# Three more products joined two by two in a nested Strassen-Winograd feed-forward

## The chip, the cores and the metric

The kernel runs on one core of a Trainium2 chip. The metric is the device time of one execution in microseconds; before the change the median of three runs is 378.93 us (378.29 to 379.14).

## What is computed

```python
def _attn_ref(q, k, v):                       # 8 batches, 12 heads, 448 tokens, 64 wide
    scores = np.matmul(q, k.transpose(0, 1, 3, 2)) / np.sqrt(q.shape[-1])
    attn = np.exp(scores - np.max(scores, axis=-1, keepdims=True))
    attn = attn / (np.sum(attn, axis=-1, keepdims=True) + 1e-09)
    return np.matmul(attn, v)

def _moe_ref(x, w_in, w_out):                 # x: 3584 x 768, w_in: 768 x 2048, w_out: 2048 x 768
    h = x @ w_in
    g = h * (1.0 / (1.0 + np.exp(-h)))
    return g @ w_out
```

The attention's output, heads side by side, is the x of the second function.

## The kernel before

**Stages.** Attention runs over 24 units of four heads. The first feed-forward product gives G, the gated hidden values, with 128 hidden columns on the partitions in each of 16 blocks f. For batches 0 to 3 it is done batch by batch with tanh gates, for the pairs of batches 4, 5 and 6, 7 by Winograd's seven products (`pair_product`, tiles `f`, three 448-column matmuls per product) with sums `sx` of x and `tw` of w_in; ScalarE then writes G with Silu. The second product, G times w_out, is done over 28 tiles of 128 tokens, two at a time: a *quad* qd holds tiles 2qd and 2qd+1, and there are 14 (0 to 13).

**A quad** is again Winograd: tokens in two tiles, hidden blocks in two halves of eight, output columns in two halves of 384 (`OH`). Its seven products (`product`, L924) take eight 128x384 matmuls each. Products 1, 2, 4 and 7 take G itself or sums written over it, products 5, 6 and 3 take sums S that VectorE makes (`combine_g`, L907, two halves of 128x512 each: S5, S6, G7, S3). The right sides are w_out or its differences D4, D5, D6. Products 1, 6, 7 and 4 share one PSUM bank and 5 and 3 another (`BANK`, L920): the bank goes on adding while readings of it are taken. ScalarE copies the bank after 1, 5, 6 and 4 into four fp32 outputs (`take_copy`, L1005), and VectorE adds the bank to them after 2, 7 and 3 (`take_sum`, L1023), which completes an output and stores it. So product 5 goes into two outputs: into (1,1), which is completed by 7, and, because product 3 is added on top of it in its bank, into (0,1), which is completed by 3.

**Joined products.** Product m of two quads a and b is twice a 128 x 1024 by 1024 x 384 product with the same right side. `FOLD` (L255) lists where both are taken together as one 2 x 2 problem with seven products of quarter size (`fold_product`, L1086): four 128x192 matmuls each, 28 in place of two times eight 128x384 ones. The price is four sums of the left sides (`fold_x`, L1064, tiles `fold`), four sums of the right side once for each m (`fold_w`, L1055, tiles `right` and others), and five readings of two banks P and Q (`fold_read`, L1109) in place of two readings. Before the change product 4 is joined for quads 7 and 8, 10 and 11, and 12 and 13, and product 2 for 10 and 11. A pair in `AHEAD_OF` runs before its quads' other products; its first readings are then copies by ScalarE (readings 1, 6, 5), and its result is added at the end by `take_last` (L1018). Entries of `FOLD` from index `MID` = 2 on take ordinary banks m for P and Q, the first two take the two double banks s that the scores used before.

**What sets the order.** The order of all engines is worked out while the program is built, by a list scheduler (`Order`, L111). Each operation has a duration written into the code, and `start` (L133) frees VectorE after that duration less `OVERLAP` (0.07). VectorE takes the ready operation with the smallest sum of ready time and bias: readings have -4, S sums 0, x and weight sums 1. TensorE takes the first entry of the list `moe` that is ready (`moe_ready`, L1938, which looks at 80 entries); quads stand in it in their order, each product as eight entries (`queue_quad`, L1796), and a joined product as seven (`queue_fold`, L1702). Buffers are counted as rings: four banks m, two or three s, three S tiles (`sg_ring`), and the output tiles of a quad (`home_of`, L1277: quads 8 and 10 use `wide` tiles, 11 others of that kind, 12 four `ost` tiles, 13 old xT tiles). `plan_sums` (L1618) plans S sums quad by quad once all of the quad's gates are known, `plan_folds` (L1657) the sums of joined products. On the chip each engine follows its queue in that order and waits for what is not there yet.

Quads 7 to 9 lie between the two pairs, from 280 us on; quads 10 to 13 need the last pair and run from 336 us to the end. The last product is product 2 of quad 13, in two halves of 192 columns (`p_2` and `p_2r`).

Of the kernel before, what the change touches and what calls it, by code (L numbers as in the profile page):

```python
# [9 lines left out]
FP16 = mybir.dt.float16  # L10
# [204 lines left out]
def kernel(  # L215
# [36 lines left out]
    FAR = (NT * B // 4 - 1,)  # L252
    BROAD = NT * B // 4 - 3
    WIDE = (NT * B // 4 - 6, NT * B // 4 - 4)
    FOLD = ((10, 11, (2, 4)), (12, 13, (4,)), *((7, 8, (4,)),))  # L255
    MID = 2
    AHEAD_OF = ((1, 4),)
    LEAD = 0
    TAIL = None
    folded = {(q, m) for a, b, ms in FOLD for q in (a, b) for m in ms}  # L260
# [645 lines left out]

    def combine_g(qd, m, f0, f1):  # L907
        a, b = 2 * qd, 2 * qd + 1
        if m != 7 and (qd, m) not in S_t:
# [8 lines left out]
        nc.vector.tensor_tensor(out=dst[:, f0:f1], in0=x[:, f0:f1], in1=y[:, f0:f1], op=op)  # L918
# [2 lines left out]

    half_t = {}

    def product(qd, m, f0, f1, strips, c0=0, c1=OH):  # L924
        w = {1: rows(2 * qd, 0), 2: rows(2 * qd, 1), 4: rows(2 * qd + 1, 1), 7: rows(2 * qd + 1, 0)}
        w = w[m] if m in w else S_t[(qd, m)]
        if BANK[m] == m and f0 == 0:
            pr_t[(qd, m)] = psum_bank(f"p_{qd}_{m}" + "r" * (c0 > 0))
        if c1 - c0 < OH:
            half_t[c0] = pr_t[(qd, m)]  # L930
        for f in range(f0, f1):
            times(
                pr_t[(qd, BANK[m])][:, 0 : c1 - c0],
                w[:, f, :],
                W_[m][:, f, c0:c1],
                f == 0 and BANK[m] == m,
                f == HF - 1,
                strips,
            )
# [70 lines left out]
    def take_end(p, c0, c1):  # L1010
# [3 lines left out]
        for lo, eng in ((0, nc.sync), (64, nc.scalar)) if c0 else ((0, nc.sync),):  # L1014
            hi = lo + 64 if c0 else 128
            eng.dma_start(out=out[row + lo : row + hi, c0:c1], in_=t[lo:hi])

    def take_last(qd):  # L1018
        t = ost_t[(qd, *OUT[4])]
        nc.vector.tensor_tensor(out=t, in0=bank(qd, 1), in1=t, op=ALU.add)  # L1020
        store(qd, *OUT[4])
# [7 lines left out]
    x2_t, n2_t = {}, {}  # L1029

    def left(q, m, k):
        return rows(2 * q + m // 4, 1)[:, 4 * k : 4 * k + 4]

    def right(m, k, j):
        return W_[m][:, 4 * k : 4 * k + 4, OH // 2 * j : OH // 2 * (j + 1)]
# [72 lines left out]

    def fold_read(g, m, k):  # L1109
        a, b = FOLD[g][:2]  # L1110
        i, j = {2: SUM[2], 4: OUT[4]}[m]
        bank = n2_t[(g, m, "P" if k in (1, 6, 7) else "Q")]
        q = b if k in (7, 5) else a
        if (g, m) in AHEAD_OF and k in (1, 5):
            ost(q, i, j)
        t = ost_t[(q, i, j)]
        if (g, m) in AHEAD_OF and k in (1, 6, 5):
            at = slice(0, OH) if k == 5 else slice(OH // 2 * (k // 6), OH // 2 * (k // 6 + 1))
            nc.scalar.copy(out=t[:, at], in_=bank[:, 0 : at.stop - at.start])
            return  # L1120
        if k in (1, 6):
            at = slice(OH // 2 * (k // 6), OH // 2 * (k // 6 + 1))
            nc.vector.tensor_tensor(out=t[:, at], in0=bank[:, 0 : OH // 2], in1=t[:, at], op=ALU.add)
        elif k == 7:
            v = t.rearrange("p (j n) -> p j n", j=2)
            nc.vector.tensor_tensor(
                out=v,
                in0=bank[:, 0 : OH // 2].unsqueeze(1).to_broadcast([128, 2, OH // 2]),
                in1=v,
                op=ALU.add,  # L1130
            )
            if (g, m) not in AHEAD_OF:
                store(b, i, j)
        else:
            nc.vector.tensor_tensor(out=t, in0=bank[:, 0:OH], in1=t, op=ALU.add)
            if k == 2 and (g, m) not in AHEAD_OF:
                store(a, i, j)
# [121 lines left out]
    def take_bank(name):  # L1259
        bank_of[name] = m_ring.take()  # L1260
# [357 lines left out]
    def plan_sums():  # L1618

        if not quads:  # L1620
            return
        qd, todo = quads[0]
        if len(todo) == 4:
            gates = {}
            for f in range(NFF):
                gates[f] = gates_at(2 * qd, f) + gates_at(2 * qd + 1, f)
                if None in gates[f]:
                    return
            gates_of[qd] = gates
# [22 lines left out]
        if not todo:  # L1652
            quads.pop(0)
# [3 lines left out]
    def plan_folds():  # L1657

        last = PAIRS[1]
        if "w" not in w2_op and last_pair and e_ring.can(1, od.now):  # L1660
            w2_op["w"] = True
            e_slot["spare"] = e_ring.take()
            for m in (4, 2):
                for i in (1, 2, 3, 4):
                    more = [w2_op[(m, i // 2)]] if i in (2, 4) else []
                    w2_op[(m, i)] = od.add(
                        Op("DVE", 0.57, lambda m=m, i=i: fold_w(m, i), last_pair + more, 1)
                    )
        if not folds or "w" not in w2_op:
            return  # L1670
        g, m, done = folds[0]
        made = [x for q in FOLD[g][:2] for f in range(HF, NFF) for x in gates_at(2 * q + m // 4, f)]
        n = len(x2_op) // 4
        if g < MID:
            if (last, HF - 1) not in pair_done:
# [26 lines left out]
    def queue_fold(g, m):  # L1702
# [1 line left out]
        done, reads = {}, {}  # L1704
        fold_done.append(done)
        folds.append((g, m, done))
        first = {2: 1, 4: 4}[m]
        early = (g, m) in AHEAD_OF
        if early:
            ahead[a] = lambda: when([reads.get(2)])  # L1710
            ahead[b] = lambda: when([reads.get(7)])
        home = {q: home_of(q) for q in (a, b)}

        def read(k, busy, deps, then=None):
# [4 lines left out]
        def queue(k):  # L1719
# [48 lines left out]
            def deps():  # L1768
# [15 lines left out]
                if not i:  # L1784
# [11 lines left out]
    def queue_quad(qd):  # L1796
# [16 lines left out]
        def queue(m, f0, f1, c0=0, c1=OH):  # L1813
            first = {6: (1,), 2: (1,), 7: (6, 5), 3: (5, 6) if qd == LAST else (5, 6, 7), 4: (7,)}.get(m, ())

            def run():
# [7 lines left out]
                if BANK[m] == m and f0 == 0:  # L1824
                    take_bank(f"p_{qd}_{m}" + "r" * (c0 > 0))
                for ring, need in rings:
                    ring.take(need)
                if m in (5, 6, 3) and f1 == HF:
# [8 lines left out]
                    od.add(Op("DVE", 0.33, fn, [op, took[1]], -4))  # L1837
                    return
                pr_op[(qd, m)] = op
                read(m, [op] + [took[x] for x in {2: (1,), 7: (5,), 3: (6,)}.get(m, ())])  # L1840
                if m == 7 and (qd, 4) in folded:
                    if qd in ahead:
                        def then(at):
                            leave_bank(f"p_{qd}_1")(at)
                            home.give(at + STORE)
# [6 lines left out]
                                [op, took[7], ahead[qd]],  # L1852
                                -4,
                                then=then,
                            )
# [4 lines left out]
            def deps():  # L1860
# [4 lines left out]
                made += [took.get(x) if x in hard else (took.get(x), 9.0) for x in first]  # L1865
                if m in (1, 2, 4):
                    t = 2 * qd + m // 4
                    i = int(m != 1)
# [6 lines left out]
            rings = ((home, 1),) if f0 == 0 and (m in OUT or m == 7 and (qd, 4) in folded and qd not in ahead) else ()  # L1875
            moe.append((deps, int(BANK[m] == m and f0 == 0), run, rings))


        begun = {}
# [460 lines left out]
```

## Time and profile before

| | |
|---|---|
| median of three runs | 378.93 us |
| the profiled execution | 378.17 us |
| its span, first to last instruction | 376.4 us |
| granted TensorE clock | 1.000 |
| TensorE busy | 370.2 us, 98% |
| VectorE busy | 287.5 us, 76% |
| ScalarE busy | 255.6 us, 68% |
| chain that ended last | PE 95%, ACT 3%, DMA 1% |

PE is TensorE's matmuls, PEld its weight loads, DVE is VectorE, ACT ScalarE, POOL GpSimd and SP the queue that issues most stores. The page divides the span into 40 slices of 9.4 us and gives the busy share of each engine in tenths. In lists in order of time a line merges equal instructions: start, length from the first start to the last end, engine, line, output and inputs, shape and count; an idle time in front of it and what ended it stand in brackets. Instructions of one engine overlap, so that the distance from one start to the next is shorter than the length of a line that holds one instruction.

### The profile page before, as it was taken

To read this page: it belongs to the slowest core of one execution; us is meant where nothing else is said; L and a number is where in the kernel's file an instruction comes from. 1 tells how busy PE (TensorE), PEld (TensorE's weight loads), DVE (VectorE), ACT (ScalarE), POOL (GpSimd) and SP (SyncE) were. 2 spreads that over 40 slices of the span, in tenths; PEclk is the share of its full clock that TensorE was granted. 3 is DMA by queue.
4 is the path that set the end of the run, shared out by engine and by line. 5 is a ranking of instruction groups with operands and counts; after the bars stand their busy time and mean duration, and the time that the engine had idled before them with its cause. 6 is when DMAs were issued, how large, how long until landed. Compare 5 with 4: busy or idle time off the path is not lost.

```text
span 376.4 us, 9978 instructions
## 1 busy us (share of the span) xinstructions
PE 370.2 (98%) x4030; PEld 188.0 (50%) x4030; DVE 287.5 (76%) x597; ACT 255.6 (68%) x401; POOL 85.0 (23%) x155
## 2 busy tenths in 40 slices
PE   7999999999999999999999999999999999999996
PEld 3365445444444444444444454545556655556764
DVE  3668858999995969995969998899379725449853
ACT  4988873896878787877788777658872238883130
POOL 6653337424016326006423200000000000000000
PEclk9999999999999999999999999999999999999999
DMA  7999999919049849147954411210002240001334
GB/s 113 198 208 209 207 200 181 205 21 132 16 96 153 154 51 123 27 94 108 176 91 67 57 46 44 55 32 0 0 3 53 74 108 20 0 1 34 84 96 126
DMA packets 35966, 34.47 MB, mean 92 GB/s; under 512 B 11856, under 2 KB 35152, under 8 KB 35920
## 3 DMA queue, kind: packets, MB, share of 16 engines
q0 software_dynamic: 25312, 22.82, 40.9%
q1 hardware_dynamic: 10064, 10.38, 10.1%
q10 hardware_dynamic: 544, 0.64, 0.5%
q8 instruction: 31, 0.51, 0.5%
q14 instruction: 15, 0.12, 0.1%
HBM read 45.61 MB, written 11.01 MB: 150 GB/s over the span
## 4 chain that ended last, share of the span: by engine, by line
PE 95%; ACT 3%; DMA 1%; DVE 0%; issue 0%; POOLq 0%
PE p L685 29%; PE h L685 21%; PE f L685 16%; PE s L448 11%; PE a L570 8%; PE o L685 3%; ACT E L504 2%; PE a L556 2%; PE a L603 2%; PE n_Q L685 1%; PE n_P L685 1%; DMA rk<-in_k_dram 1%; ACT T L493 1%; PE z L685 0%; PE p_2r L685 0%
## 5 line engine op out<-in xcount | busy, mean ns | idle before, releaser
L504 ACT ACTIVATE E<-s 128x896 f16<-128x896 f32 x164 | 141.9, 921 | 24.5 <-PE s L448 24.5
L685 PE MATMUL h<-xT,w_in_t 128*32 128x448 f16 (+2 forms) x762 | 83.5, 348 | 0.0
L685 PEld LDWEIGHTS <-w_in_t 128*128 128x128 f16 (+1 forms) x909 | 54.6, 97 | 50.0 <-issue 8.0
L354 POOL DMA_DIRECT2D V<-in_v_dram x88 | 48.5, 560 | 51.2 <-PE a L570 29.2
L685 PEld LDWEIGHTS <-G 128*128 128x128 f16 (+1 forms) x668 | 41.9, 97 | 28.0 <-issue 5.2
L717 ACT ACTIVATE th<-h 128x448 f16<-128x448 f32 x67 | 36.6, 546 | 24.2 <-PE h L685 20.7
L685 PE MATMUL p<-w_out_t,G 128*128 128x384 f16 (+2 forms) x326 | 51.8, 324 | 0.0
L448 PE MATMUL s<-rq,KT 32*128 32x448 f16 (+3 forms) x728 | 44.9, 347 | 1.4 <-DVE rq L412 0.9
L685 PEld LDWEIGHTS <-S 128*128 128x128 f16 (+1 forms) x321 | 29.5, 98 | 22.3 <-issue 3.4
L761 DVE SCALAR_TENSOR_TENSOR G<-th,h 128x448 f16<-128x448 f16 (+1 forms) x64 | 35.7, 573 | 4.8 <-ACT th L717 4.3
L685 PE MATMUL p<-D,S 128*128 128x384 f16 (+1 forms) x217 | 39.0, 326 | 0.0
L1006 ACT COPY ost<-p 128x384 f32<-128x384 f32 x38 | 18.2, 480 | 24.6 <-PE p L685 16.2
L570 PE MATMUL a<-E,V 128*32 128x448 f16 (+1 forms) x640 | 32.7, 356 | 0.0
L1025 DVE TENSOR_TENSOR ost<-p,ost 128x384 f32<-128x384 f32 x29 | 16.0, 553 | 18.4 <-ACT ost L1006 9.6
L673 DVE SCALAR_TENSOR_TENSOR xT<-a,rdn 128x448 f16<-128x448 f32 x46 | 27.0, 619 | 3.0 <-PE a L570 2.4
L334 POOL DMA_DIRECT2D rq<-in_q_dram x25 | 13.9, 559 | 67.3 <-PE s L448 57.9
L448 PEld LDWEIGHTS <-KT 32*128 32x128 f16 (+1 forms) x824 | 12.3, 96 | 31.5 <-issue 29.8
L517 DVE TENSOR_TENSOR T<-T,E 128x1792 f16<-128x1792 f16 x21 | 22.8, 1086 | 4.7 <-ACT E L504 4.7
L888 DVE TENSOR_TENSOR p<-f,p 128x448 f32<-128x448 f32 x15 | 9.4, 624 | 22.2 <-PE f L685 12.3
L517 DVE TENSOR_TENSOR T<-E,E 128x1792 f16<-128x1792 f16 x21 | 22.8, 1084 | 4.0 <-ACT E L504 4.0
L685 PE MATMUL f<-sx,tw 128*128 128x448 f16 x102 | 23.4, 352 | 0.0
L570 PEld LDWEIGHTS <-V 128*32 128x32 f16 (+1 forms) x640 | 13.5, 95 | 18.0 <-issue 10.1
(134 smaller groups left out, 464.5 us busy)
## 6 DMA issues: line engine op xcount, KB each, us to landing
out_dram<-ost SPq DMA_DIRECT2D x147, 48.0 KB, 1.8
rk<-in_k_dram POOLq DMA_DIRECT2D x24, 224.0 KB, 5.4
rq<-in_q_dram POOLq DMA_DIRECT2D x23, 224.0 KB, 5.7
w_out_t<-in_moe_w_out_dram POOLq DMA_DIRECT2D x4, 768.0 KB, 13.5
V<-in_v_dram POOLq DMA_DIRECT2D x42, 64.0 KB, 4.0
out_dram<-wide SPq DMA_DIRECT2D x48, 48.0 KB, 1.6
V<-in_v_dram POOLq DMA_DIRECT2D x42, 48.0 KB, 4.4
w_in_t<-in_moe_w_in_dram POOLq DMA_DIRECT2D x6, 256.0 KB, 8.7
```

What stands on the lines that cost most here:

```text
L334: nc.gpsimd.dma_start(out=rawq[n][:, cols], in_=group_of(q, b, hg)[:, cols])
L354: nc.gpsimd.dma_start(out=VT[b][32 * x : 32 * (x + 1), hs, at : at + count, :], in_=v[b, hs].rearrange("h (i g) d -> i h g d", g=TPP)[:, : ...
L448: nc.tensor.matmul(out=pS[p0 : p0 + 32 * (x1 - x0), h % 2, at : at + q1 - q0], lhsT=KT[(b, hg)][32 * h : 32 * (h + 1), key_rows(b, hg, c, ...
L504: nc.scalar.activation(out=E[(n, w)][:, 2 * y : 2 * y + 2, :], in_=pS_t[(n, w, y)][:, :, 0:S], func=AF.Exp, scale=attn_scale,)
L517: nc.vector.tensor_tensor(out=T[n], in0=T[n] if step else E[(n, 0)], in1=E[(n, step + 1)], op=ALU.add,)
L570: nc.tensor.matmul(out=a[32 * h : 32 * (h + 1), 0:S], lhsT=VT[b][k0:k1, HG * hg + h, place(b, hg, c), part - 1 :: 2], rhs=e[k0:k1, h], sta ...
L673: nc.vector.scalar_tensor_tensor(out=x3(b, cc)[:, cc % 3, 32 * g0 : 32 * g1], in0=acc[(n, part)][:, 0:nq], scalar=0.5, in1=rdn_t[n].rearra ...
L685: nc.tensor.matmul(out=out[i : i + cut], lhsT=w[:, i : i + cut], rhs=x, start=start, stop=stop, skip_group_check=True,)
L717: nc.scalar.activation(out=th, in_=h_t[(b, f, t0)][:, 0:n], func=AF.Tanh)
L761: nc.vector.scalar_tensor_tensor(out=dst[:, f, at + lo : at + hi], in0=th_t[(b, f, t0)][:, lo - t0 : hi - t0], scalar=1.0, in1=h_t[(b, f, ...
L1006: nc.scalar.copy(out=ost(qd, *OUT[m]), in_=bank(qd, BANK[m]))
L1025: nc.vector.tensor_tensor(out=t, in0=bank(qd, BANK[m]), in1=t, op=ALU.add)
```

## The change

`FOLD` gets product 5 of quads 10 and 11, product 5 of quads 12 and 13, and product 2 of quads 8 and 9 (a new entry with index 3). Both products 5 run ahead of their quads.

- Sums S5 of quads 10 to 13 do not take a tile S any more but an old tile of 448 columns by four heads: that of `tw_4_4`, `tw_3_0`, `tw_4_0` and `sx_6_3` (sums that the last pair's products read). They take no place in `sg_ring`.
- The sums of the right side for m = 5 are written over columns 0 to 767 of w_in, planned when the last pair's blocks f = 0 to 5 have all been multiplied.
- With 5 joined, product 3 opens its own bank (`opens`). The result of the joined product lies in output (1,1); `take_mix` adds it on VectorE to output (0,1), which the copy after product 6 has filled. Readings 7 and 3 wait for that.
- Durations that the planner charges: an S sum after the scores are done 0.35 instead of 0.40, an x sum 0.36 instead of 0.43.

```diff
-    FOLD = ((10, 11, (2, 4)), (12, 13, (4,)), *((7, 8, (4,)),))
+    FOLD = ((10, 11, (5, 2, 4)), (12, 13, (5, 4)), (7, 8, (4,)), (8, 9, (2,)))
     MID = 2
-    AHEAD_OF = ((1, 4),)
+    AHEAD_OF = ((0, 5), (1, 5), (1, 4))
...
+        if m == 5 and (qd, 5) in folded:
+            slot = e_slot[{10: "tw_4_4", 11: "tw_3_0", 12: "tw_4_0", 13: f"sx_{PAIRS[1]}_3"}[qd]]
+            if (qd, m) not in S_t:
+                t = sb.tile([128, HG, S], FP16, name=f"S_{qd}_{m}", tag=f"E{slot}", bufs=1)
...
+    def opens(qd, m):
+        return BANK[m] == m or m == 3 and (qd, 5) in folded
...
+    def take_mix(qd):
+        t = ost_t[(qd, *OUT[6])]
+        nc.vector.tensor_tensor(out=t, in0=t, in1=ost_t[(qd, *OUT[5])], op=ALU.add)
...
+        if m == 5:
+            return w_in_t[:, i - 1, 0 : 2 * OH].rearrange("p (f n) -> p f n", f=4)
...
-        while todo and (todo[0] == 7 or sg_ring.can(1, od.now)):
+        while todo and (todo[0] == 7 or (qd, todo[0]) in folded or sg_ring.can(1, od.now)):
             m = todo.pop(0)
-            if m != 7:
+            if m != 7 and (qd, m) not in folded:
                 sg_ring.take()
...
-                            0.40,
+                            0.40 if qk_seq else 0.35,
...
+        if "five" not in w2_op and (last, 5) in pair_done:
+            made = [pair_done[(last, f)].get(m) for f in range(6) for m in range(1, 8)]
+            if None not in made:
+                w2_op["five"] = True
+                for i in (1, 2, 3, 4):
+                    more = [w2_op[(5, i // 2)]] if i in (2, 4) else []
+                    w2_op[(5, i)] = od.add(Op("DVE", 0.57, lambda i=i: fold_w(5, i), made + more, 1))
...
-                Op("DVE", 0.43, lambda i=i: fold_x(g, m, i, homes[i - 1]), made + more, 1)
+                Op("DVE", 0.36, lambda i=i: fold_x(g, m, i, homes[i - 1]), made + more, 1)
...
-                read(m, [op] + [took[x] for x in {2: (1,), 7: (5,), 3: (6,)}.get(m, ())])
+                read(m, [op] + [took[x] for x in {2: (1,), 7: (5,), 3: (6,) + (5,) * ((qd, 5) in folded)}.get(m, ())])
+                if m == 6 and (qd, 5) in folded:
+                    took[5] = od.add(
+                        Op("DVE", OH / 960.0 + 0.13, lambda: take_mix(qd), [took[6], ahead[(qd, 5)]], -4)
+                    )
```

More of the change, by code (lines that the diff above doesn't have):

```diff
@@ L908, in combine_g @@
         a, b = 2 * qd, 2 * qd + 1
-        if m != 7 and (qd, m) not in S_t:
+        if m == 5 and (qd, 5) in folded:
+            slot = e_slot[{10: "tw_4_4", 11: "tw_3_0", 12: "tw_4_0", 13: f"sx_{PAIRS[1]}_3"}[qd]]
+            if (qd, m) not in S_t:
+                t = sb.tile([128, HG, S], FP16, name=f"S_{qd}_{m}", tag=f"E{slot}", bufs=1)
+                t = t.rearrange("p h s -> p (h s)")[:, 0 : 128 * HF]
+                S_t[(qd, m)] = t.rearrange("p (f t) -> p f t", f=HF)
+        elif m != 7 and (qd, m) not in S_t:
             S_t[(qd, m)] = sb.tile([128, HF, 128], FP16, name=f"S_{qd}_{m}", tag="S", bufs=NSG)
@@ L926, in product @@
         w = w[m] if m in w else S_t[(qd, m)]
-        if BANK[m] == m and f0 == 0:
-            pr_t[(qd, m)] = psum_bank(f"p_{qd}_{m}" + "r" * (c0 > 0))
+        if opens(qd, m) and f0 == 0:
+            pr_t[(qd, BANK[m])] = psum_bank(f"p_{qd}_{BANK[m]}" + "r" * (c0 > 0))
         if c1 - c0 < OH:
@@ L935, in product @@
                 W_[m][:, f, c0:c1],
-                f == 0 and BANK[m] == m,
+                f == 0 and opens(qd, m),
                 f == HF - 1,
@@ L1031, in left @@
     def left(q, m, k):
-        return rows(2 * q + m // 4, 1)[:, 4 * k : 4 * k + 4]
+        x = S_t[(q, 5)] if m == 5 else rows(2 * q + m // 4, 1)
+        return x[:, 4 * k : 4 * k + 4]
     def right(m, k, j):
@@ L1110, in fold_read @@
         a, b = FOLD[g][:2]
-        i, j = {2: SUM[2], 4: OUT[4]}[m]
+        i, j = {2: SUM[2], 4: OUT[4], 5: OUT[5]}[m]
         bank = n2_t[(g, m, "P" if k in (1, 6, 7) else "Q")]
@@ L1671, in plan_folds @@
         g, m, done = folds[0]
-        made = [x for q in FOLD[g][:2] for f in range(HF, NFF) for x in gates_at(2 * q + m // 4, f)]
+        if m == 5:
+            made = [x for q in FOLD[g][:2] for x in sg_op.get((q, 5), [None])]
+        else:
+            made = [
+                x for q in FOLD[g][:2] for f in range(HF, NFF) for x in gates_at(2 * q + m // 4, f)
+            ]
         n = len(x2_op) // 4
@@ L1706, in queue_fold @@
         folds.append((g, m, done))
-        first = {2: 1, 4: 4}[m]
+        first = {2: 1, 4: 4, 5: 5}[m]
         early = (g, m) in AHEAD_OF
         if early:
-            ahead[a] = lambda: when([reads.get(2)])
-            ahead[b] = lambda: when([reads.get(7)])
+            ahead[(a, m)] = lambda: when([reads.get(2)])
+            ahead[(b, m)] = lambda: when([reads.get(7)])
         home = {q: home_of(q) for q in (a, b)}
@@ L1783, in deps @@
                     made.append(w2_op.get((m, i)))
-                if not i:
+                if m == 5 and k in (1, 2, 4):
+                    made += sg_op.get((b if k == 4 else a, 5), [None])
+                elif not i:
                     q = b if k == 4 else a
@@ L1823, in run @@
                 )
-                if BANK[m] == m and f0 == 0:
-                    take_bank(f"p_{qd}_{m}" + "r" * (c0 > 0))
+                if opens(qd, m) and f0 == 0:
+                    take_bank(f"p_{qd}_{BANK[m]}" + "r" * (c0 > 0))
                 for ring, need in rings:
@@ L1839, in run @@
                 pr_op[(qd, m)] = op
-                read(m, [op] + [took[x] for x in {2: (1,), 7: (5,), 3: (6,)}.get(m, ())])
+                read(m, [op] + [took[x] for x in {2: (1,), 7: (5,), 3: (6,) + (5,) * ((qd, 5) in folded)}.get(m, ())])
[3 more added lines that the diff above has]
+                    )
                 if m == 7 and (qd, 4) in folded:
-                    if qd in ahead:
+                    if (qd, 4) in ahead:
                         def then(at):
@@ L1851, in run @@
                                 lambda: take_last(qd),
-                                [op, took[7], ahead[qd]],
+                                [op, took[7], ahead[(qd, 4)]],
                                 -4,
@@ L1864, in deps @@
                 hard = {6: (1,), 7: (6,), 3: (5,), 4: (7,)}.get(m, ())
-                made += [took.get(x) if x in hard else (took.get(x), 9.0) for x in first]
+                made += [
+                    took.get(x) if x in hard else (took.get(x), 9.0)
+                    for x in first
+                    if x != 5 or (qd, 5) not in folded
+                ]
                 if m in (1, 2, 4):
@@ L1873, in deps @@
                 return made + [x[0], (x[1], 4 * mm(OH))]
-            rings = ((home, 1),) if f0 == 0 and (m in OUT or m == 7 and (qd, 4) in folded and qd not in ahead) else ()
-            moe.append((deps, int(BANK[m] == m and f0 == 0), run, rings))
+            rings = ((home, 1),) if f0 == 0 and (m in OUT or m == 7 and (qd, 4) in folded and (qd, 4) not in ahead) else ()
+            moe.append((deps, int(opens(qd, m) and f0 == 0), run, rings))
         begun = {}
```

## The prediction

> **What bounds the kernel now.** I read the engines' busy shares and the slices first, then the busy time by stages, then the instructions in order of time of TensorE and VectorE in the last 40 us. The first two views:
>
> ```profile
> PE 370.2 (98%) x4030; PEld 188.0 (50%) x4030; DVE 287.5 (76%) x597; ACT 255.6 (68%) x401; POOL 85.0 (23%) x155
> PE   7999999999999999999999999999999999999996
> DVE  3668858999995969995969998899379725449853
> ```
>
> TensorE bounds it: 98% overall and 9 in every slice but the first and the last. So a product that becomes shorter shortens the kernel, as long as nothing makes TensorE wait. VectorE's 76% is an average; its slices 36 and 37 (338.7 to 357.5 us) show 9 and 8. That is the stage of quads 10 to 13, where most of the change falls. By stages (columns: span, then busy time and instructions of PE, PEld, DVE, ACT, POOL):
>
> ```profile
> 280.00:299.70 19.70, 19.70 (x137) 12.78 (x136) 18.72 (x48) 4.73 (x11) 0.00 (x0) 1.00 0.21 54
> 299.70:307.60 7.90, 7.90 (x50) 4.72 (x49) 1.70 (x4) 1.60 (x4) 0.00 (x0) 1.00 0.42 106
> 330.00:336.10 6.10, 6.10 (x34) 3.17 (x33) 2.23 (x4) 5.08 (x11) 0.00 (x0) 1.00 0.00 0
> 338.76:350.60 11.84, 11.84 (x81) 7.54 (x79) 11.79 (x34) 3.40 (x8) 0.00 (x0) 1.00 0.14 35
> 350.60:363.70 13.10, 13.10 (x118) 10.22 (x117) 10.27 (x26) 2.77 (x8) 0.00 (x0) 1.00 0.35 91
> 338.76:373.00 34.24, 33.99 (x259) 23.55 (x256) 26.10 (x68) 7.59 (x17) 0.00 (x0) 1.00 0.30 82
> ```
>
> Here TensorE never waits, the granted clock is 1.00 throughout, and VectorE has no idle time from 338.76 to 350.60 us (11.79 of 11.84). From 338.76 to the end it has 34.24 - 26.10 = 8.1 us free, of which 9.30 - 4.04 = 5.3 us lie after 363.70, behind the last products (stage 363.7 to 373: 4.04 us busy).
>
> **What is removed: 0.92 us of TensorE.** The price of both forms of a product, in order of time:
>
> ```profile
> 354.47 0.49 PE L685 MATMUL n_Q<-right,G 128*128 128x192 f16 x4
> 354.80 0.49 PE L685 MATMUL n_P<-T,fold 128*128 128x192 f16 x4
> 355.13 0.49 PE L685 MATMUL n_Q<-T,fold 128*128 128x192 f16 x4
> ...
> 363.47 2.76 PE L685 MATMUL p<-D,S 128*128 128x384 f16 x16
> 366.07 1.46 PE L685 MATMUL p<-w_out_t,S 128*128 128x384 f16 x8
> ```
>
> Starts count, not the durations, which overlap. Four 192-column matmuls take 0.33 us (354.47 to 354.80 to 355.13; 0.3275 over longer rows), sixteen 384-column ones 2.60 (363.47 to 366.07). A joined product is 7 x 0.3275 = 2.29 in place of 2.60: 0.31 saved, three times: 0.92.
>
> A rule speaks against this. The Trainium skill ("TensorE: Matmul & The Clock Gate", section "LDWEIGHTS (loading the stationary operand)") prices a weight load by its 128 columns at 128 / 1.2 = 107 ns, whatever streams past it; if loads set the pace, an estimate from it is 28 x 0.107 = 2.99 us for a joined product, 0.39 more than 2.60, and three would cost 1.16 instead of saving 0.92. The trace shows 82 ns per 192-column matmul, each with its own weights, so I keep 0.92 in the sum.
>
> **What is added on VectorE.** Prices are from start to start, since each instruction overlaps the one before:
>
> ```profile
> 337.20 0.42 DVE L918 TENSOR_TENSOR S<-G 128x512 f16<-128x512 f16 x1
> 338.76 0.43 DVE L918 TENSOR_TENSOR S<-G 128x512 f16<-128x512 f16 x1 [1.14 <-ACT G L896]
> 339.10 0.42 DVE L1084 TENSOR_TENSOR fold<-G 128x512 f16<-128x512 f16 x1
> 339.44 0.76 DVE L918 TENSOR_TENSOR S<-S,X 128x512 f16<-128x512 f16 x2
> 340.11 0.42 DVE L918 TENSOR_TENSOR G<-X,G 128x512 f16<-128x512 f16 x1
> ...
> 351.43 0.56 DVE L1025 TENSOR_TENSOR wide<-p,wide 128x384 f32<-128x384 f32 x1 [0.79 <-PE p L685]
> 351.91 0.55 DVE L1135 TENSOR_TENSOR wide<-n_Q,wide 128x384 f32<-128x384 f32 x1
> 352.37 0.41 DVE L918 TENSOR_TENSOR S<-G,S 128x512 f16<-128x512 f16 x1
> ```
>
> A 128x512 sum takes 0.335 (338.76 to 339.10 to 339.44), a 128x384 read of PSUM 0.47 (351.43 to 351.91 to 352.37), a 128x192 read 0.27 (348.22 to 348.49), a 128x768 sum of weights 0.47 (281.44 to 281.91).
>
> *Weights of product 5*: 4 x 0.47 = 1.9 us, allowed once the last pair's f = 5 has been multiplied (about 330 us). From 330.00 to 336.10 VectorE is busy 2.23 of 6.10, so they lie in idle time: 0. Their inputs are needed by nothing before 338.8.
>
> *Quads 8 and 9, product 2*: four sums (1.34) and five reads (2 x 0.27 + 3 x 0.47 = 1.95) instead of two reads (0.94): 2.35 us more. The sums fall where VectorE has 1.0 us left in 19.7; the reads fall after 299.70, where 6.2 of 7.9 us are idle. What hides the fold's own waits (read 1 before product 6, read 6 before 7) is product 4 of quad 9 and the pair product at 304.33. Bounds 0 and 0.35 of wait (one narrow read, 348.22 to its end); I take 0.1.
>
> *Quads 10 to 13, product 5*: eight x sums (2.68), four wide reads (1.88; reads 1, 6 and 5 go to ScalarE, which is busy 7.59 of 34.24 and loses four copies of 0.48), and four take_mix. A take_mix adds two fp32 tiles in SBUF, which no row shows; the nearest rows are the 128x384 read with one side in PSUM (0.47) and a 16-bit sum of 384 columns at the rate of the 512 one (0.25). I take 0.47, the row of the same width and type; four are 1.9 (at the least 1.0). Sum: 6.4 us. The S5 sums stay; two are merely held back for their new homes: S5 of quad 10 now overwrites the tile of weights that the last pair product reads until 338.15, so its first half moves from 337.20 to 338.2, into the 1.14 us in which VectorE idled anyway: 0.
>
> So VectorE has 26.1 + 6.4 = 32.5 us to do in 34.24 - 0.62 = 33.6 us, and 5.3 of the old idle time lie where only the last reads can go. That is no longer hidden for certain.
>
> **The step that I price highest.** The order is written by a planner, and the change also lowers what the planner charges: a S sum 0.35 (0.40 before), an x sum 0.36 (0.43). Order.start takes 0.07 off (OVERLAP), so it counts 0.28 and 0.29 from start to start; the rows say 0.335. With 0.33 the old plan was right, and TensorE shows no wait in this stage. In the new plan each sum runs 0.05 us late on the chip. The x sums of the first joined product 5 (quads 10 and 11) are the worst place: its entries stand first in the list, so the planner gives them to TensorE the moment it thinks them ready. Before its last x sum stand about 24 sums: S5, S6, G7 and S3 of quads 10 and 11 (15 after 338.76), S5 of 12 (2), three x sums of product 2, four of its own; until take_mix no reads come between. Lateness 24 x 0.05 = 1.2, less 0.1 margin that the planner leaves at the last gate (it counts 0.20 + 0.56 + 0.10 = 0.86 us from the last pair product to the sum behind it, the rows 0.78, 337.98 to 338.76). In TensorE's in-order queue everything waits behind that matmul: 1.1 us. Bounds: 0 (if other work is placed ahead and VectorE catches up) and 1.3.
>
> The second half (quads 12, 13) has some 24 more sums, so up to 1.2 more; VectorE idled 2.8 us there (13.10 - 10.27), and TensorE runs late itself by then, which gives the sums time. Bounds 0 and 1.2; I take 0.2.
>
> **Sum.** -0.92 + 0.1 + 1.1 + 0.2 = +0.48 us, on the profiled execution's 378.17 (span 376.4, 1.8 around it): 378.65. The median shown is 378.93, 0.76 above that execution; on it the forecast is 379.4. The end is the same: the last product is still product 2 of quad 13 in two halves.
>
> **Rivals.**
>
> 1. *The cover holds.* The free 8.1 us are enough and the plan is not too eager: -0.92, or 378.0. For it: VectorE's totals still fit (32.5 of 33.6), and TensorE was dense at 11.79 of 11.84. Against it: the 0.05 us per sum. Chance 0.22.
>
> 2. *The banks close* (slower). Read 7 and read 3 of quads 10 and 11 add onto outputs that take_mix must have filled, and take_mix needs the whole joined product 5 read. Until then p_10_1, p_11_1 and both banks of product 3 stay taken: all four banks, and both s tiles are with the joined product. Nothing of quad 12 can open. The chain from its last matmul is 0.2 until a reader starts (366.07 to 366.27 in the copy of a p), two reads 0.94, mix 0.47, read 0.47, about 2.1 us before a bank comes free; TensorE holds the two opening products of the next join (0.66) and what is left of product 3. It decides from the point at which the join ends after the other six products (7.8 us, from 338.3 to about 348). Price 2.1 - 0.66 = 1.4, once here and once for 12 and 13, and it takes the place of the lateness above, since the join's end sets both: -0.92 + 2.8 = +1.9, or 380.8. Against it: the list is greedy and may run the join earlier. Chance 0.35.
>
> 3. *Weight loads set the pace*: the page of the profile gives 98 ns for one; 28 x 0.098 = 2.74, 0.14 over 2.60, three +0.43, with the stalls above +1.8: 380.8. Against it are the rows at 354 us. It is what the section of the Trainium skill named above would make of it. Chance 0.03.
>
> The forecast has 0.40. A measurement of this kernel tells 0.2% (0.76 us) from no change. Of rival 1, 0.19 is beyond that on the fast side and 0.03 within; of the forecast (378.6 to 379.9), 0.36 within and 0.04 slower; of rival 2, 0.03 within and 0.32 slower; rival 3 slower. That is faster 0.19, same 0.42, slower 0.39. The likeliest case's own range is 378.6 to 379.9; for 8 in 10 the range goes from 378.0 to 380.8.
>
> **What would show it.** Right: TensorE waits in the stage from 338 us for `fold` tiles written at L1084, about 1 us in all, first at n_Q or n_P of product 5; VectorE without idle time there to about 352. Wrong: no TensorE wait and the last matmul 0.9 us earlier (rival 1); waits of p of quad 12 for a read of a bank (rival 2); starts of n_ matmuls over 82 ns apart (rival 3). A wait near 300 to 308 us would make the 0.1 wrong, a pair product late near 331 us the 0 for the weights.

## The result, and the profile after

The changed kernel takes 381.15 us (median of six, 380.87 to 381.30) against 378.98 us: 2.2 us more by the medians. The ratio of the two is estimated at 1.0065, 95% interval 1.0053 to 1.0078, which is 2.0 to 3.0 us. The two profiled executions have spans of 379.4 and 376.4 us; that of the kernel before (378.17 us) lies 0.8 below its median, so the profiles differ by more than the medians. Busy shares and slices of the changed kernel:

```profile
PE 371.8 (98%) x4066; PEld 189.8 (50%) x4066; DVE 297.3 (78%) x624; ACT 255.6 (67%) x403; POOL 85.0 (22%) x155
PE   8999999999999999999999999999999999999995
DVE  3667859989995969995969999797489544569984
```

TensorE is still at 98%, and at 9 in every slice but the first and the last, and its busy time has risen although its work fell by 0.92 us. Busy time hides short waits here: a matmul counts as busy until its modelled end, some 0.17 us after the next could have started (one 384-column matmul is 0.33 long, and the next starts 0.16 behind it). So I compare starts: from one line's start to the next, less the count times 0.1625 us (384 columns) or 0.0819 us (192). Lines with a wait, of TensorE after the change, in order of time (records of a few matmuls are missing from each trace, which such sums must leave out):

```profile
297.69 0.33 PE L685 MATMUL p<-D,S 128*128 128x384 f16 x1
298.25 0.49 PE L685 MATMUL n_Q<-D,fold 128*128 128x192 f16 x4 [0.23 <-DVE wide L1151]
...
345.16 0.50 PE L685 MATMUL n_Q<-w_in_t,fold 128*128 128x192 f16 x4 [0.43 <-DVE fold L1100]
345.50 1.46 PE L685 MATMUL p<-D,S 128*128 128x384 f16 x8
346.80 0.49 PE L685 MATMUL p<-w_out_t,G 128*128 128x384 f16 x2
347.51 0.51 PE L685 MATMUL n_P<-w_in_t,fold 128*128 128x192 f16 x4 [0.22 <-DVE fold L1100]
```

From 297.69 to 298.25 one matmul of 0.16 us ran: 0.40 us were lost where the bracket says 0.23. From 346.80, two matmuls (0.325) and a loss of 0.38 lead to 347.51. Added up so, TensorE loses 1.06 us at quads 7 to 9 (288 to 302 us), 0.10 behind the last pair, 1.56 at the first joined product 5 (340 to 350 us) and 0.67 later (356 to 361). The sum is 3.39; less the 0.92 saved, the last matmul should start 2.47 later.

The start-up varies by up to 1.7 us between the profiled executions, so I measure from the first matmul of quad 7 on (279.92 before, 279.84 after). The second half of the last product (the *last half* from here on) starts 92.01 us behind it before and 94.58 after, 2.57 later. What follows that start, the *tail*, is 4.4 and 4.9 us. VectorE in the two stages that had shown 11.79 of 11.84 and 10.27 of 13.10 us:

```profile
338.55:350.60 12.05, 11.14 (x79) 6.83 (x78) 11.18 (x32) 3.82 (x10) 0.00 (x0) 1.00 0.00 0
350.60:363.70 13.10, 12.84 (x112) 9.70 (x111) 12.93 (x35) 2.74 (x7) 0.00 (x0) 1.00 0.32 81
363.70:376.00 12.30, 11.54 (x102) 8.72 (x99) 8.80 (x19) 2.24 (x6) 0.00 (x0) 1.00 0.51 146
```

Its free time went from the second stage (12.93 of 13.10), and its work in the last rose from about 4 to 8.8 us. The last figures of the first row are those of the DMA engines: 0.00 and 0 GB/s. No store leaves before 350.6; before the change they left from 344.52 on. The queue of SP, before and then after (start, length, count):

```profile
344.52 17.59 SPq L999 DMA_DIRECT2D out_dram<-wide  x32
363.28 8.33 SPq L999 DMA_DIRECT2D out_dram<-ost  x7
372.55 1.09 SPq L1016 DMA_DIRECT2D out_dram<-ost  x2
```

```profile
351.82 16.40 SPq L1008 DMA_DIRECT2D out_dram<-wide  x32
368.54 5.87 SPq L1008 DMA_DIRECT2D out_dram<-ost  x7
375.01 1.13 SPq L1025 DMA_DIRECT2D out_dram<-ost  x2
```

The 32 `wide` stores are quads 10 and 11. Their outputs now wait for the joined product, so they start 7.3 us later, take half a us each, and run almost without a gap into the stores of quads 12 and 13.

Yet the last store is not issued late. ScalarE's queue issues it; that ends 1.78 us after the start of the last half, against 1.79 before. Its landing is late: the last three stores land 2.5 to 2.8 us after their issue, against 1.9 to 2.1 before. From 4 us ahead of that start on, the DMA engines have 1.38 MB to move, against 1.18.

### The profile page after: what moved, and what is told of

Read it like the earlier page. It is cut to its first block, busy times and chain, and to the rows that moved or that the text cites. A ratio compares the mean times of both kernels' runs of the same rounds, so it can differ in the third digit from the quotient of the medians.

```text
span 379.4 us, 10067 instructions
## 1 busy us (share of the span) xinstructions
PE 371.8 (98%) x4066; PEld 189.8 (50%) x4066; DVE 297.3 (78%) x624; ACT 255.6 (67%) x403; POOL 85.0 (22%) x155
## 4 chain that ended last, share of the span: by engine, by line
PE 89%; DVE 7%; ACT 1%; DMA 1%; issue 1%; DVEq 0%; POOLq 0%
PE p L685 23%; PE h L685 21%; PE f L685 16%; PE s L448 11%; PE a L570 8%; PE o L685 3%; DVE S L924 3%; PE a L556 2%; PE a L603 2%; PE n_Q L685 2%; DVE fold L1100 1%; DMA rk<-in_k_dram 1%; PE n_P L685 1%; DVE G L924 1%; ACT T L493 1%
## 5 line engine op out<-in xcount | busy, mean ns | idle before, releaser
L685 PE MATMUL p<-w_out_t,G 128*128 128x384 f16 (+2 forms) x310 | 49.5, 324 | 0.0
L685 PEld LDWEIGHTS <-S 128*128 128x128 f16 (+1 forms) x313 | 28.1, 98 | 19.6 <-issue 3.4
L1015 ACT COPY ost<-p 128x384 f32<-128x384 f32 x36 | 17.3, 480 | 26.1 <-PE p L685 18.1
L685 PE MATMUL p<-D,S 128*128 128x384 f16 (+1 forms) x185 | 34.1, 327 | 0.0
```

The costliest lines, as they stand in the source:

```text
L685: nc.tensor.matmul(out=out[i : i + cut], lhsT=w[:, i : i + cut], rhs=x, start=start, stop=stop, skip_group_check=True,)
L1015: nc.scalar.copy(out=ost(qd, *OUT[m]), in_=bank(qd, BANK[m]))
```

## The experiments

Two theories to begin with. *Lateness*: the plan charges VectorE too little. *Capacity*: VectorE has too much to do, whatever the plan believes. "Old charges" is this edit, in the changed kernel:

```diff
-                            0.40 if qk_seq else 0.35,
+                            0.40,
-                Op("DVE", 0.36, lambda i=i: fold_x(g, m, i, homes[i - 1]), made + more, 1)
+                Op("DVE", 0.43, lambda i=i: fold_x(g, m, i, homes[i - 1]), made + more, 1)
```

The first four runs: that edit; its reverse in the kernel before; and with it, `FOLD` cut to the join of 8 and 9, or to the joins of 5.

> The changed kernel with the planner's old charges for the sums (S 0.40, x 0.43), all three joins kept. Lateness theory (the plan counts 0.28 to 0.29 us per sum, VectorE takes 0.335, so TensorE's queue meets sums that are not there): nearly all of the 3.4 us of gaps between TensorE's starts goes, to at most 0.7; time 377.9 to 378.9. Capacity theory (VectorE simply has too much to do, whatever the plan believes): gaps stay at 2 us or more, time 380 to 381.3.

> The kernel before with nothing changed but the two lower charges. Lateness theory: no work is added, yet TensorE gets gaps, at quads 7 to 9 first (about 0.5 to 1 us there) and some at quads 10 to 13; time 379.6 to 380.8. Capacity theory: nothing to speak of, 378.8 to 379.2.

> Old charges, only the join of product 2 of quads 8 and 9 added. Lateness theory: 0.3 less than before, 378.5 to 378.9. Capacity theory: VectorE had 1.0 us free in 280.0 to 299.7 and gets 1.3 us of sums there, so TensorE waits 0.3 to 1 us: 379.0 to 379.8.

> Old charges, only the two joins of product 5 (with take_mix) added, none for quads 8 and 9. Lateness theory: 0.6 less than before, with up to 0.4 of waits for the tightest sums, 378.3 to 378.9. Capacity theory: the 6.4 us added to VectorE after 338 us do not fit before the last products, 379.8 to 381.

The table has all runs; times are ratios to the kernel before on the same chip. "Start" is that of the last half behind quad 7's first matmul. The last three columns are us from that start on: to the end of the last store's issue, to the end of the span (the tail), and to an instruction packet, of which more below; "none" says that there is none from 10 us before it to the end. All of them come from one profile each; profiles of one kernel differ too, so a ratio with its interval goes first where the two disagree.

| run | ratio (95%) | start | last store | tail | packet |
|---|---|---|---|---|---|
| before | 1 | 92.01 | 1.79 | 4.4 | none |
| the change | 1.0065 (1.0053 to 1.0078) | 94.58 | 1.78 | 4.9 | -4.3 |
| old charges | 1.0035 (1.0022 to 1.0048) | 92.51 | 2.51 | 5.5 | -2.5 |
| charges alone | 1.0008 (0.9997 to 1.0019) | 92.29 | 1.78 | 4.4 | none |
| join 8, 9 | 1.0007 (0.9994 to 1.0020) | 92.07 | 1.79 | 4.4 | none |
| both joins of 5 | 1.0040 (1.0026 to 1.0054) | 92.42 | 3.12 | 6.1 | -0.9 |
| ... mix on GpSimd | 1.0110 (1.0083 to 1.0137) | 96.86 | 1.78 | 4.5 | -3.9 |
| ... stores of 12 by GpSimd | 1.0145 (1.0121 to 1.0170) | 92.52 | 2.33 | 9.6 | -0.9 |
| join of 5, 10 and 11 | 1.0041 (1.0026 to 1.0056) | 92.71 | 1.78 | 6.3 | 2.7 |
| join of 5, 12 and 13 | 0.9996 (0.9980 to 1.0012) | 91.91 | 1.78 | 4.4 | none |
| both, stores of 10, 11 split | 1.0037 (1.0022 to 1.0053) | 92.42 | 2.51 | 5.5 | -1.4 |
| ... and 12 off ScalarE | 1.0041 (1.0025 to 1.0057) | 92.63 | 3.33 | 5.9 | -1.3 |
| three joins, the same stores | 1.0049 (1.0033 to 1.0065) | 92.63 | 3.16 | 5.8 | -1.3 |
| joins 8, 9 and 12, 13 | 1.0002 (0.9992 to 1.0012) | 92.02 | 1.78 | 4.4 | -2.9 |
| join of 10, 11, stores split | 1.0023 (1.0014 to 1.0032) | 92.71 | 1.78 | 4.4 | none |
| both, split, no mix | 1.0050 (1.0037 to 1.0062) | 92.92 | 2.86 | 5.2 | -0.7 |
| before, stores held to 353 | 1.0045 (1.0033 to 1.0058) | 92.01 | 3.75 | 6.1 | none |
| before, stores held to 357 | 1.0136 (1.0120 to 1.0151) | 92.02 | 7.12 | 9.5 | none |

Neither theory came through whole. With the old charges TensorE starts the last half 2.1 us earlier (92.51 for 94.58) and its waits for `fold` are gone; that is lateness, shown. Its lost starts fall from 3.4 to 1.3 us, between the two expectations. But the time falls by 0.30% only (1.1 us), in part because the tail grows by 0.5 us, and the kernel stays slower than before. On the 378.93 us from which the expectations were made, 1.0035 is 380.3: inside the range of capacity, as is the time with the joins of 5 alone (380.4).

The charges alone cost nothing that can be measured, against what I expected of lateness. Idle time is not what covers them: from 340.2 to 352.0 us VectorE is busy 11.65 of 11.80 us in that run, and TensorE loses no start there. What that run lacks is the first joined product 5, the consumer right behind its sums; that this is the reason fits, but no run shows it by itself. And the join of 8 and 9, given its place by the old charges, costs nothing that can be measured and gains nothing: it saves 0.31 and loses 0.34 (0.27 at 293, 0.07 at 302 us).

So the cost without the charges is that of the joins of 5, and most of it is tail (6.1). Four runs on which join, and what in it. Their edits to the run with both joins of 5, in the order of the four expectations (shortened; the first also gives GpSimd a queue in the plan):

```diff
-        nc.vector.tensor_tensor(out=t, in0=t, in1=ost_t[(qd, *OUT[5])], op=ALU.add)
+        nc.gpsimd.tensor_tensor(out=t, in0=t, in1=ost_t[(qd, *OUT[5])], op=ALU.add)
-                        Op("DVE", OH / 960.0 + 0.13, lambda: take_mix(qd), [took[6], ahead[(qd, 5)]], -4)
+                        Op("GP", 0.9, lambda: take_mix(qd), [took[6], ahead[(qd, 5)]], -4)
...
+            eng = nc.gpsimd if qd == LAST - 1 else nc.scalar if turn % 2 and 4 * qd + 8 >= NT * B else nc.sync
...
+    FOLD = ((10, 11, (5, 2, 4)), (12, 13, (4,)), (7, 8, (4,)))
+    AHEAD_OF = ((0, 5), (1, 4))
+                if (g, m) == (1, 4) and k in (1, 4):
+                    made.append(fold_done[1].get(2))
...
+    FOLD = ((10, 11, (2, 4)), (12, 13, (5, 4)), (7, 8, (4,)))
+    AHEAD_OF = ((1, 5), (1, 4))
```

> As the run with the joins of 5 alone (old charges, ratio 1.0040), but the four take_mix are done by GpSimd, which is idle there, and charged 0.9 us. Theory A (VectorE's load: its 6.4 us more push its readings to the end): 1.9 us go from VectorE, the tail behind the last matmul falls from 6.2 to about 5, ratio 1.000 to 1.002. Theory B (the chain join, mix, reading holds the end, whoever mixes): a slower mix lengthens it, ratio 1.004 to 1.007.

> As the run with the joins of 5 alone, but the stores of quad 12 that SP or ScalarE issued are issued by GpSimd's queue. Theory C (the stores that now bunch up in SP's queue, some 0.8 us each, make the longer tail): the tail falls from 6.2 to 4.5 to 5.2, ratio 1.000 to 1.002. Theory A (VectorE's readings themselves are late): the tail falls by 0.6 at most, ratio 1.0025 to 1.004.

> Old charges; only the join of product 5 of quads 10 and 11 is added, and the join of product 4 of 12 and 13 may begin only after it (otherwise both wait for the other's bank). If the cost comes from the end (the join of 12 and 13 is read last, with nothing behind it): no cost here, 0.3 saved, ratio 0.9985 to 1.0005. If each join of 5 costs by VectorE's load wherever it stands: ratio 1.0015 to 1.003.

> Old charges; only the join of product 5 of quads 12 and 13 is added. If the cost comes from the end: nearly all of it, ratio 1.003 to 1.005, with TensorE's wait for ScalarE's copy near 367 us and a tail of 5.5 us or more. If each join costs by VectorE's load: ratio 1.0015 to 1.003.

I had put the cost at the end, and it is the other way round: the join of 12 and 13 costs nothing that can be measured, and the join of 10 and 11 alone costs as much as both. Part of that is no tail: TensorE loses 0.78 us at 352.34, waiting for a copy by ScalarE.

GpSimd is no help, and both runs with it are above every expectation. Two mixes keep it 2.13 us; TensorE then loses 1.29 us at 353 and 2.21 at 371 us, and behind the second wait its granted clock is 0.50 from 372 to 374 us and 0.55 to 375.2, so part of that run's 1.0110 is the clock. Stores that GpSimd issues among the last make the tail 9.6: the last store lands at 378.11, but GpSimd's closing drain lasts until 381.33.

What sets the join of 10 and 11 apart, I thought, is its stores. In its run VectorE's last readings have gaps as before the change, so they are not the cause. Half of these 32 stores went to GpSimd's queue, early, in the first three of the next four runs; the second edit is in two of them:

```diff
+            if qd in (10, 11) and turn % 2:
+                eng = nc.gpsimd
...
-            eng = nc.scalar if turn % 2 and 4 * qd + 8 >= NT * B else nc.sync
+            eng = nc.scalar if turn % 2 and qd == LAST else nc.sync
```

> As the run with the joins of 5 alone (ratio 1.0040, tail behind the last matmul 6.2 us), but every second store of quads 10 and 11 is issued by GpSimd's queue, early, where nothing waits for it. Store theory (joining 10 and 11 ahead delays their 32 stores by 7 us, SP issues them at half a us each up to 369 us and the last stores meet them): tail 4.4 to 5.0, ratio 0.999 to 1.001. Load theory (VectorE's late readings make the tail): tail 5.7 or more, ratio 1.003 to 1.0045.

> As the run before it, and the stores of quad 12 that ScalarE's queue issued are issued by SP. Store theory, second part (ScalarE's copy of a joined product stands behind a store that waits for take_mix, so TensorE waits 0.7 us near 367 us): that gap is gone, 0.7 us less than the run before it, ratio 0.997 to 1.000. Load theory: the gap stays, since the copy waits for VectorE; no less.

> All three joins with the old charges (ratio 1.0035 so far) and both changes of the stores. Store theory: TensorE's saving of 0.92 less the gaps near 300 us (0.4): 0.5 us faster than before, ratio 0.997 to 1.000. Load theory: 1.002 to 1.0035.

> Old charges and old stores; the joins of 8 and 9 and of 12 and 13, but not that of 10 and 11. Store theory: no tail, no join whose outputs hold back 32 stores; the two savings of 0.31 less 0.4 to 0.5 of gaps, ratio 0.998 to 1.0005. Load theory (each join costs by VectorE's time): 1.001 to 1.0025.

With both joins of 5 the store theory fails in its numbers. The tail falls by 0.6, not by 1.7. With quad 12's stores moved to SP, TensorE's wait for the copy is not gone (0.94 us at 369.97, where 0.72 stood at 368.15), and the last store is issued 0.8 later. Three joins with both changes are slower than either theory said (1.0049). Only the joins of 8, 9 and 12, 13 came in as the store theory had it (1.0002). Then the join of 10 and 11 alone with the same split, and both joins with the split and without the mixes (edit: `lambda: None` for `take_mix`, charged 0.08):

> The join of 10 and 11 alone (ratio 1.0041, tail behind the last matmul 6.3 us, its readings at the end spaced out as before the change), with every second store of quads 10 and 11 issued by GpSimd. If these 32 late stores make its tail: tail 4.4 to 5.0, what is left is TensorE's +0.7 us, ratio 1.0005 to 1.0025. If the tail has another cause: tail 5.8 or more, ratio 1.0035 to 1.0045.

> As the run with both joins of 5 and the stores of 10 and 11 split (ratio 1.0037, tail 5.6), but the four take_mix are left out, so output (0,1) of quads 10 to 13 lacks product 5; readings keep their order otherwise. If what is left of the cost is VectorE's load (readings back to back from 370.5 to the end): 1.9 us less on VectorE, readings at the end spaced out, tail 4.4 to 4.9, the gap near 368 us gone, ratio 0.998 to 1.001. If it is not VectorE's load: ratio 1.0025 to 1.004.

For the join of 10 and 11 alone the split gives the numbers of the store theory. SP without and with it:

```profile
351.56 15.33 SPq L1008 DMA_DIRECT2D out_dram<-wide  x28
366.99 0.37 SPq L1008 DMA_DIRECT2D out_dram<-ost  x1
367.46 1.76 SPq L1008 DMA_DIRECT2D out_dram<-wide  x4
369.33 4.10 SPq L1008 DMA_DIRECT2D out_dram<-ost  x6
```

```profile
351.82 11.12 SPq L1010 DMA_DIRECT2D out_dram<-wide  x14
363.05 0.38 SPq L1010 DMA_DIRECT2D out_dram<-ost  x1
363.52 0.90 SPq L1010 DMA_DIRECT2D out_dram<-wide  x2
367.80 5.03 SPq L1010 DMA_DIRECT2D out_dram<-ost  x6
```

SP is through with `wide` at 364.4 instead of 369.2, the tail is 4.4 instead of 6.3, and the ratio 1.0023 is about what TensorE's start (0.7 us later) leaves. But that does not prove the theory. The two ratios' intervals overlap. The profiled execution without the split, 380.96 us, is 1.05 above its kernel's median, so its tail is longer than usual. And its last store is issued as early as with the split (1.78 us).

What differs is the landing of the last stores, and for that there is a rival that I had not considered. The profile has a DMA queue q8 of kind "instruction". Without the split a packet of 16 KB starts on it at 375.60 and takes 1.17 us; with the split there is none. From 373.5 us to the end without the split, and from 373.7 to 377.5 with it (the packet's count, MB and share; then a store's size and the us to its landing):

```profile
q8 instruction: 1, 0.02, 1.3%
out_dram<-ost SPq DMA_DIRECT2D x1, 96.0 KB, 4.3
```

```profile
out_dram<-ost SPq DMA_DIRECT2D x1, 96.0 KB, 2.0
```

Without the split the last three stores land 3.8 to 4.3 us after their issue, with it 1.9 to 2.1, although from 376.40 to 378.20 the DMA engines are busy only 3% of the time and so, taken together, are not short of room. The kernel before has the same in the middle: a packet on q8 starts at 357.58, and the four stores issued from 356.33 on land after 3.4, 3.1, 2.8 and 2.5 us, the other `wide` ones after 1.5 to 2.1. In the table, every run with a tail above 5 us has such a packet between 2.5 us before and 2.7 us after the start of the last half, or is one of the two runs below that hold stores back; no other run has one there. In the run with both joins of 5, stores issued just before the packet land after 3.5 to 3.8 us, and ScalarE's last store waits for one of these landings (374.86) before it goes out at 374.95. So the tails of the joins may come from late stores, from the instruction packet that falls among them, or from both: no run moves the packet alone.

Nor is VectorE's load shown to be out of it: without the four mixes the kernel is no faster (1.0050), but that run has a longer wait of its own, 1.23 us where 0.72 stood. There TensorE waits for a copy on ScalarE, which stands behind a store in its own queue (ScalarE's queue, then TensorE):

```profile
366.49 0.57 ACTq L1010 DMA_DIRECT2D out_dram<-ost  x1
367.55 0.32 ACT L1137 COPY ost<-n_P 128x192 f32<-128x192 f32 x1 [3.43 <-DVE ost L1040]
```

```profile
366.53 0.33 PE L685 MATMUL p<-w_out_t,S 128*128 128x384 f16 x1
367.92 0.49 PE L685 MATMUL n_P<-T,fold 128*128 128x192 f16 x4 [1.06 <-ACT ost L1137]
```

The store is of an output that VectorE completes at L1040, and ScalarE's copy of the joined product's first sum comes behind it: 1.23 us from start to start.

The last test leaves all joins out. In the kernel before, only the order of SP's queue is changed: stores of quads 10 and 11 are kept back until one late output of theirs is stored, (0,0) or (1,0).

```diff
     def store(qd, i, j):
+        if qd in (10, 11) and "open" not in held_back:
+            if (qd, i, j) not in ((10, 0, 0), (11, 0, 0)):
+                held_back.append((qd, i, j))
+                return
+            todo = [(qd, i, j)] + held_back
+            held_back.append("open")
+            for x in todo:
+                store_now(*x)
+            return
+        store_now(qd, i, j)
```

> The kernel before, no join added and no instruction of TensorE, VectorE or ScalarE touched: only the 32 stores of quads 10 and 11 are held back in SP's queue until the first output of their joined product 2 is there, near 353.3 us instead of 344.5. SP then issues them until about 370 us. Store theory: the last matmul starts where it did, the tail behind it grows from 4.5 by 0.5 to 1.8 us, ratio 1.001 to 1.004. If late stores are not what lengthens the end: ratio 0.999 to 1.001.

> The same, held until the first output of their joined product 4, near 357.1 us; SP issues them until about 374. Store theory: every 4 us more of delay adds nearly all of it, since SP has no gap left: tail 6 to 9, ratio 1.005 to 1.011. Otherwise 0.999 to 1.001.

The queue of SP in the first of them:

```profile
352.99 15.76 SPq L1013 DMA_DIRECT2D out_dram<-wide  x32
370.27 3.94 SPq L1013 DMA_DIRECT2D out_dram<-ost  x7
374.31 1.08 SPq L1030 DMA_DIRECT2D out_dram<-ost  x2
```

The last half starts at 92.01, where it did, and yet the kernel is 0.45% slower (1.7 us), and 1.36% (5.1 us) with 4.3 us more delay; both are above the store theory's range. No packet on q8 is near, and here the issue is late: the last store's ends after 3.75 and 7.12 us instead of 1.79. So stores that reach SP too late lengthen the end by themselves, and from there on 4.3 us of delay cost 3.4. That is settled.

It does not settle the joins, because the delay here is larger than theirs. Counted back from the start of the last half, the 32 stores begin 27.4 us ahead before, 22.6 in the change, 21.3 with the join of 10 and 11 alone, 19.7 with both joins of 5, and 18.7 in the first of these two runs. In the change and with the join of 10 and 11 alone SP has caught up in time, and the last store leaves as before.

## Why the prediction was wrong

Its time was 379.4 with a range to 380.8; it was 381.15. The mechanism of its largest term came true; its sizes failed, that of quads 8 and 9 above all, and so did the end, which it put at nothing. In the two profiles the last half starts 2.57 us later and the tail is 0.50 longer, 3.07 in place of the sum's 0.48. By its own steps:

- *What is removed, 0.92 us*: right. Four 192-column matmuls are 0.33 us apart in the new places too (345.16 to 345.50). The Trainium skill's price for a weight load ("TensorE: Matmul & The Clock Gate", "LDWEIGHTS (loading the stationary operand)") gives an estimate of 0.43, if loads set the pace; the trace does not agree.
- *What is added on VectorE, 6.4 us*: right in sum. In 338.76 to 378 us it is busy 32.9 us, against 32.5 forecast. A take_mix is 0.46 from start to start (351.98 to 352.44).
- *The weights of product 5 for nothing*: right; they run at 330.1 to 331.6 and at 334.1 us, and the pair products keep their 0.57.
- *The step priced highest, 1.1 us at the first joined product 5*: right in mechanism and place, 1.56 measured, in four waits from 340.80 to 349.52. The x sum that product 5 of the join needs starts at 344.69 and takes 0.41; TensorE starts at 345.16.
- *Quads 8 and 9, 0.1 us*: mis-sized, 1.06, the largest error of the sum. I charged the lateness to quads 10 to 13 alone, though the same charge plans the sums of quads 7 to 9, and the stage had 1.0 us of VectorE free, which I had read out. The join alone costs 0.34 of waits and the charges alone 0.14; both together 1.06.
- *The second half, 0.2 us*: wrong in place. TensorE loses 0.67 us between 356 and 361 us, but still in products 2 and 4 of quads 10 and 11 (the largest, 0.36, waits for a reading by VectorE); from quads 12 and 13's joined product 5 on it loses nothing. With the old charges these waits are gone, which fits lateness, and another of 0.72 for ScalarE's copy stands at 368.76.
- *No term at all*: 0.10 behind the last pair.
- *"The end is the same"*: the last product is the same, but the tail, put at nothing, grew by 0.50. I followed the joined product's chain to the banks (rival 2), where nothing waited: quad 12 opened its banks without a gap. The same chain, join, mix, reading, ends in the stores, and I never asked when they would start: 7.3 us later. In the change the last store is still issued in time, and only lands later; whether the bytes that now come late or the instruction packet at 370.14 does that is open.
- *Rival 1* failed: TensorE waits, and the end is longer. *Rival 2* failed: no product p of quad 12 waited for a reading. *Rival 3* failed: the spacing stayed.

Of the 2.0 to 3.0 us, the lower charges cost about 1.1 in this kernel, which the run with the old charges shows. About 1.3 stay with the old charges. By the runs that take the joins one by one they come with the join of 10 and 11: in part as waits for ScalarE's copies, in part as tail, and the cause of that tail stays open.

Open too: with both joins of 5 and the stores of 10 and 11 split, the tail is still 5.5 us. Quads 12 and 13 then deliver their outputs after 366 us, ScalarE's copies stand behind stores there, and an instruction packet falls among the last stores; no run separates these. No version tried is faster than the kernel before beyond its interval; the nearest is the join of 12 and 13 alone, 0.9996 (0.9980 to 1.0012).

## What to carry to other kernels

A product that is moved ahead holds back every output that waits for its result: follow the outputs to the queue that stores them, count its stores and their issue time, and ask when the first can go (8.5 us of delay for 32 stores cost 1.7 us with all else unchanged). When a tail is longer, look first whether its last store was issued late or landed late, and what else the DMA engines moved then. A planner's charge that is a little too low may cost nothing by itself and over 1 us with added work, so price the two together, in every stage that the charge plans. On an engine that is always busy, add up starts, since busy time and idle brackets take some 0.17 us off every wait.

## What the runs showed of the hardware

- With take_mix on GpSimd (two in 350.55 to 352.68), two x sums on VectorE at 350.88 took 2.09 us together, against 0.75 for two elsewhere. Three readings of PSUM beside the other two mixes (366.67 to 368.72) took 1.61, against about 1.5 elsewhere.
- SP issues a 48 KB store of 32 rows every 0.5 us (32 in 16.40 us); such stores land 1.6 us after issue when nothing else is in the way.
- Stores in flight around a 16 KB packet of the instruction queue land up to 2.3 us later than others: 4.3 instead of 2.0 us for the 96 KB store in the run of the join of 10 and 11.
- ScalarE's queue holds compute behind a store that waits for another engine: 1.23 us of TensorE in one place.
- After a wait of 2.05 us (until 371.39, mixes on GpSimd) the granted clock is 0.77 from 371.3 to 372 us, 0.50 to 374 and 0.55 to 375.2, then 1.00 again. After the wait of 1.13 us at 353.29 in the same run the matmuls keep their spacing.
- GpSimd's closing drain in the run with quad 12's stores on its queue lasts from 374.19 to 381.33, 3.2 us beyond the last landing.
